# Four edits to the order of transfers and VectorE work in a spectral mixer and token MLP with its backward pass

## The chip, the cores and the metric

The kernel runs on one core of one Trainium2 chip. A core has a matrix engine (TensorE, PE in the profile), a vector engine (VectorE, DVE), a scalar engine (ScalarE, ACT), a general engine (GpSimd, POOL) and a sequencer for transfers (SyncE, SP; its queue is SPq). All transfers of this kernel are issued by SP, in the order of its program: where SP waits before one of them, all later ones wait too. The metric is the device time in microseconds (us) of one execution, lower is better.

## The reference

One layer with two residual blocks, and then the gradients of everything. With x of 2048 x 448 (S x D, bf16):

```python
def _A_ref(x, w_r, w_i):
    X = rfft2(x, axes=(-2, -1))
    X = X * (w_r + 1j * w_i)
    return irfft2(X, s=(S, D)).astype(bfloat16)

def _B_ref(x, w1, b1, w2, b2):
    h = _layernorm(x)
    u = _gelu(einsum("bsd,sf->bdf", h, w1) + b1)
    y = einsum("bdf,fs->bds", u, w2) + b2
    return y.transpose(0, 2, 1)

h = x + _A_ref(_layernorm(x), A_w_r, A_w_i)
h2 = h + _B_ref(_layernorm(h), B_w1, B_b1, B_w2, B_b2)
```

The outputs are h2 and, for a given grad_out, the gradients of x, w_r, w_i (2048 x 225 each), w1 (2048 x 1792), b1, w2 (1792 x 2048) and b2.

## The kernel before

The Fourier transforms are matrix products with sine and cosine matrices that the kernel makes itself. The order of the work on PE, SP, DVE and ACT is the order of the program text; no scheduler moves it. Two helpers bend it. `fill(n)` issues up to n matmuls of a generator that stands in `pending`, so that PE has independent work in a gap. `defer(us, fn)` puts off a transfer's issue until the program has issued that much matmul time. `evac` copies a PSUM result to SBUF on ACT or DVE, whichever has the smaller sum of estimated costs so far (`Meter`).

The stages, in order:

- **Forward rows** (the loop over t up to 16): `row_a` and `row_b` make the transform along D of one row block; after every second `row_b` a reshuffle (L649, 226 KB) moves the result from the partitions of one layout to those of the next, region r2 (`D2`). In between `fill` issues products of `dg_gen`: the 14 products of w2 with grad_out, whose transposed w2 loads (L292) go through a ring of five buffers in rE and rO. From the ninth on (`CAP = 9`) these loads are held back. The loads of W (w_r and w_i, four each, L566) are spread over the last row blocks, two of them held until the next stage.
- **Forward spectrum** (`s2_stage`): 16 groups of rows are transformed along S, in eight pairs `c2`, multiplied by W on DVE (`w_mult`) and transformed back (`s2_inv`). In `make_inv` it also turns the forward matrices into the inverse ones: `gen_inv_s` (UTt, VTt) and `gen_inv_d` (csI, four transposes on PE, four scalings on ACT, four on DVE). `w_place` copies W from its load layout (rB) to the layout of the groups (rG) with `evac`. A `drain` issues what is left of `dg_gen`, then `inv_rows` and the layer norm give h.
- **MLP**: seven blocks of two (jp 0 to 6), each with 32 matmuls into u, then gelu on ACT and DVE: g into rE (`gj`), and in six more DVE operations the gelu's derivative (`om`) times dg into rD, with the sum for the gradient of b1. Then y, 16 blocks t of 14 matmuls: `y_head` for the first three up to j = 12, and `y_tail` on DVE, which adds b2 and h (loaded back from memory, L994) and stores. The results lie in a ring of four PSUM banks.
- **Backward**: 16 products with transposed w1 give dh (`ln_bwd` on ACT and DVE), with the backward rows three blocks behind (`LAG`); `fold_prep` prepares two rows on DVE for `row_a`. `gw_gen` makes the gradient of w2 out of transposed g (rE) and later that of w1 out of transposed h (rB), each read through a ring of three buffers in rst by `st_load` (L1173), stored out of a ring of three buffers in rO. These products are the `fill` of the **backward spectrum** (a second `s2_stage`). The gradient of w1 also needs du (rD) transposed, in four quarter loads (`load_du`, L1146) into r2, the region of the row spectra D2.
- **Last stage**: `inv_rows` with `gx_consumer` gives the gradient of x, while the gradients of W and of w1 are stored.

## Time and profile before

| | us |
|---|---|
| median of 3 runs | 404.02 (402.53 to 405.4) |
| profiled execution, its own time | 401.27 |
| its span (first to last instruction) | 399.5 |
| PE busy | 357.9 (90%) |
| DVE busy | 287.3 (72%) |
| ACT busy | 207.6 (52%) |
| POOL busy | 23.5 (6%) |

The chain of work that ended last consists of PE for 46% of the span, DVE for 33%, transfers for 8% and ACT for 7%. The transfers moved 81.85 MB, and the queue of SP took 81.5% of the time of the core's 16 transfer engines. In the rows of the profile L212 is the helper that issues every matmul and L78 the one that issues nearly every ACT and DVE operation, so an instruction is known by its tiles: `ps_mm<-rC,rE` is a matmul of rE (weights) with rC. Buffer numbers are left out there, so r2, r3, r452, r448 all read `r`.

### The profile page before, as it was taken

Reading aid. Unit: us, or ns where it says so; the run is one execution under the profiler, and the core shown is the slowest. Engines: PE = TensorE matmul, PEld = TensorE weight load, DVE = VectorE, ACT = ScalarE, POOL = GpSimd, SP = SyncE. Lnnn points to the kernel's source line nnn. Section 1 sums busy time; section 2 is a strip of 40 time slices with the busy share of each in tenths; the row PEclk is TensorE's granted clock in tenths of the full one; section 3 lists DMA queues with packets and bytes.
Section 4 is the critical chain, followed back from the end, with each engine's and each line's share of the span. In section 5 each row is a group of like instructions: output and inputs, shape, how many; then the busy total and the mean of one; then the engine's idle time right before and its main releaser. Section 6 shows DMA issues by size and latency. Waiting matters only on the chain.

```text
span 399.5 us, 6226 instructions
## 1 busy us (share of the span) xinstructions
PE 357.9 (90%) x2089; PEld 193.7 (48%) x2089; DVE 287.3 (72%) x737; ACT 207.6 (52%) x438; POOL 23.5 (6%) x96
## 2 busy tenths in 40 slices
PE   0888949789899999899999999899999889899795
PEld 0454626334555555445555666544554335455452
DVE  8999627981694888843249887747999923788784
ACT  4486616763896453413213444535545525777472
POOL 8600000000120000000030000000000000000000
PEclk9999989999999999999999999999999999999899
DMA  8999996337999999797858784496455989997774
GB/s 236 287 148 248 193 187 132 87 94 238 283 292 338 322 294 205 152 262 188 195 121 168 176 167 105 113 279 227 142 168 160 235 242 304 243 221 177 194 212 161
DMA packets 146249, 81.85 MB, mean 205 GB/s; under 512 B 97449, under 2 KB 140457, under 8 KB 145833
## 3 DMA queue, kind: packets, MB, share of 16 engines
q1 hardware_dynamic: 146216, 81.46, 81.5%
q8 instruction: 16, 0.26, 0.3%
q14 instruction: 17, 0.13, 0.1%
HBM read 27.56 MB, written 23.89 MB: 129 GB/s over the span
## 4 chain that ended last, share of the span: by engine, by line
PE 46%; DVE 33%; DMA 8%; ACT 7%; issue 4%; SPq 0%; POOL 0%; DVEq 0%; ACTq 0%; POOLq 0%
PE ps_mm L212 37%; DVE rS L78 10%; PE ps_ff L212 9%; DVE rG L78 6%; DVE r L78 5%; DMA rst<-rB 4%; ACT rG L78 2%; DVE rD L78 2%; DVE stats L78 2%; ACT rO L78 2%; DVE rO L78 2%; DMA out_dram<-r 2%; DMA r<-r 1%; DVE rE L78 1%; DMA rE<-in_B_w_dram 1%
## 5 line engine op out<-in xcount | busy, mean ns | idle before, releaser
L212 PEld LDWEIGHTS <-r 128*128 128x128 bf16 (+1 forms) x568 | 54.7, 106 | 44.0 <-issue 2.3
L212 PEld LDWEIGHTS <-rst 112*128 112x128 bf16 x480 | 46.0, 98 | 54.0 <-issue 6.5
L212 PE MATMUL ps_mm<-r,rst 112*128 112x512 bf16 (+1 forms) x256 | 53.2, 356 | 6.2 <-DVE rO L78 3.1
L212 PE MATMUL ps_mm<-rG,rst 112*128 112x512 bf16 x224 | 53.1, 378 | 1.4 <-DMA rst<-rE 1.4
L78 ACT CAST rO<-ps_mm 128x512 bf16<-128x512 f32 (+1 forms) x64 | 35.3, 562 | 32.5 <-PE ps_mm L212 22.9
L212 PEld LDWEIGHTS <-rS 128*128 128x128 bf16 (+1 forms) x368 | 32.2, 99 | 36.2 <-DVE rS L78 7.9
L78 DVE CAST rO<-ps_mm 128x512 bf16<-128x512 f32 (+1 forms) x56 | 35.3, 643 | 17.9 <-PE ps_mm L212 11.8
L212 PE MATMUL ps_mm<-rD,r 128*128 128x448 bf16 x224 | 44.5, 352 | 0.0
L212 PE MATMUL ps_mm<-rC,rE 128*128 128x448 bf16 x144 | 37.1, 378 | 1.6 <-DMA rE<-in_B_w_dram 1.6
L212 PE MATMUL ps_mm<-rB,r 128*128 128x448 bf16 x160 | 31.2, 352 | 0.1
L78 ACT CAST r<-ps_ff 128x452 bf16<-128x452 f32 x47 | 25.4, 540 | 7.2 <-PE ps_ff L212 7.2
L212 PE MATMUL ps_ff<-csI,rAT 113*128 113x448 bf16 x108 | 25.7, 361 | 2.1 <-ACT rAT L78 1.9
L78 DVE SCALAR_TENSOR_TENSOR r<-ps_mm,b2col,r 128x448 bf16<-128x448 f32 x16 | 10.8, 683 | 22.6 <-PE ps_mm L212 16.4
L78 ACT ACTIVATE r<-ps_mm 128x448 bf16<-128x448 f32 x16 | 8.7, 544 | 30.7 <-PE ps_mm L212 30.7
L212 PE MATMUL ps_mm<-rE,rS 128*128 128x448 bf16 x112 | 21.7, 352 | 1.1 <-DVE rE L78 1.1
L78 ACT ACTIVATE r<-rC 128x448 bf16<-128x448 bf16 x16 | 9.1, 571 | 26.0 <-DMA out_dram<-r 19.3
L78 ACT ACTIVATE rG<-rG 128x896 bf16<-128x896 bf16 x14 | 13.3, 950 | 17.4 <-DVE rG L78 17.1
L78 ACT ACTIVATE rS<-rS 128x452 bf16<-128x452 bf16 x16 | 9.3, 580 | 23.2 <-DVE rS L78 23.1
L212 PEld LDWEIGHTS <-rO 128*128 128x128 bf16 (+1 forms) x165 | 15.6, 98 | 11.3 <-ACT rO L78 0.2
L212 PEld LDWEIGHTS <-rE 128*128 128x128 bf16 x144 | 14.2, 104 | 11.8 <-issue 2.3
L212 PE MATMUL ps_mm<-rC,rO 128*128 128x448 bf16 x80 | 18.9, 352 | 0.0
L78 ACT CAST rS<-ps_ff 128x512 bf16<-128x512 f32 x27 | 15.7, 588 | 4.1 <-PE ps_ff L212 4.1
(161 smaller groups left out, 576.0 us busy)
## 6 DMA issues: line engine op xcount, KB each, us to landing
out_dram<-rO SPq DMA_DIRECT2D x14, 512.0 KB
out_dram<-rO SPq DMA_DIRECT2D x16, 448.0 KB
r<-in_B_w_dram SPq DMA_DIRECT2D x5, 1024.0 KB
r<-r SPq DMA_DIRECT2D x16, 226.0 KB
r<-r SPq DMA_DIRECT2D x32, 113.0 KB
rS<-in_B_w_dram SPq DMA_DIRECT2D x4, 896.0 KB
out_dram<-r SPq DMA_DIRECT2D x32, 112.0 KB
rO<-in_B_w_dram SPq DMA_DIRECT2D x2, 1024.0 KB
```

What stands on the lines that cost most here:

```text
L78: fn(**kw)
L212: nc.tensor.matmul(out, lhsT=lhsT, rhs=rhs, start=start, stop=stop)
```

## The change

- The row product and the reshuffle of the last row block are issued inside the loop, straight after those of the block before; the scalings of `gen_inv_d(1)`, which stood between them, go into the second pair of the spectrum stage. The two loads of w_i that stood in the loop go behind the last reshuffle; so does one w2 load more (`CAP` 8). The fill behind the rows is 20 matmuls, not 10.
- `evac` compares the sums with the cost of this copy added.
- For the last two MLP blocks the six derivative operations of each (and the copy and store of the gradient of b1) are put in a list, and up to three of them are issued behind each y tail.
- The first three transposed loads of g are issued in the dh loop, at its last three blocks, not behind it.
- Of the four quarter loads of du one is issued after every fourth group of the backward spectrum, whose part of r2 is then free, not all four after the last group.

```diff
-CAP = 9
-N_FILL_F = (6, 3, 10, 3, 24, 2)
+CAP = 8
+N_FILL_F = (6, 3, 20, 3, 24, 2)
...
     def evac(out, in_, scale=None):
-        if load[0] <= load[1]:
+        n = int(np.prod(in_.shape[1:]))
+        if load[0] + sc.cost('copy', n, False) <= load[1] + ve.cost('tensor_copy', n, in_.dtype == BF16):
...
-                    if c2 == 1:
-                        gen_inv_d(0)
+                    if c2 in (1, 2):
+                        gen_inv_d(c2 - 1)
...
-                if g_last(c2, i):
-                    after_fwd()
+                if after_fwd is not None and c2 < nh and g % 4 == 3:
+                    after_fwd(g // 4)
...
         row_b(t - 1)
+        if t == NT - 1:
+            row_b(t)
...
-        for _ in range((9, 10, 11, 12, 13, 13).count(t)):
+        for _ in range((9, 10, 11, 12).count(t)):
             next(w_loads)
...
-        if t == 15:
-            gen_inv_d(1)
         fill(N_FILL_F[1])
-    row_b(NT - 1)
...
-            for kind in "TWWTTT":
+            for kind in "TWWWWTTT":
                 if kind == "W":
                     next(w_loads)
                 elif held_w2:
                     held_w2.pop(0)()
...
+        d = Later(ve, om_ops) if jp >= NFB // 2 - 2 else ve
+        d.tensor_scalar(out=om, in0=z, scalar1=-1.0, scalar2=1.0, op0=ALU.mult, op1=ALU.add)
+        d.tensor_tensor(out=om, in0=om, in1=x2, op=ALU.mult)
+        d.tensor_tensor(out=q4(om), in0=q4(om), in1=gj, op=ALU.mult)
+        d.tensor_tensor(out=om, in0=om, in1=hh, op=ALU.add)
...
-    defer(12.0, out_gb1)
+    om_ops.append(lambda: defer(2.0, out_gb1))
...
         y_tail(t, py)
+        for _ in range(3):
+            if om_ops:
+                om_ops.pop(0)()
...
+        if t >= NT - 3:
+            st_load()
...
-    for _ in range(3):
-        st_load()
...
-    s2_stage(bwd_x, bwd_mult, 0, N_FILL_B[3], N_FILL_B[4], False, lambda: [load_du(q) for q in range(4)], 2.0 * INV_SD)
+    s2_stage(bwd_x, bwd_mult, 0, N_FILL_B[3], N_FILL_B[4], False, load_du, 2.0 * INV_SD)
```

Three places in the order of instructions. The first is SP's queue around the end of the forward rows. `r_72<-r_77` is a reshuffle, `rB<-in_A_w_r` and `rB<-in_A_w_i` are loads of W, and a transposed load from `in_B_w` is one of w2. Before, and then after:

```order
L649 DMA r_72<-r_77 16x8x904
L566 DMA rB<-in_A_w_i_dram 64x1x3600
L566 DMA rB<-in_A_w_i_dram 48x1x3600
L649 DMA r_72<-r_77 16x8x904 x2
L292 DMA_TRANSPOSE rO<-in_B_w_dram 128x16x128
L566 DMA rB<-in_A_w_i_dram 16x3375
L566 DMA rB<-in_A_w_i_dram 16x225
L292 DMA_TRANSPOSE rE<-in_B_w_dram 128x16x128 x3
```

```order
L567 DMA rB<-in_A_w_r_dram 16x225
L650 DMA r_72<-r_77 16x8x904 x3
L293 DMA_TRANSPOSE rO<-in_B_w_dram 128x16x128
L567 DMA rB<-in_A_w_i_dram 64x1x3600
L567 DMA rB<-in_A_w_i_dram 48x1x3600
L567 DMA rB<-in_A_w_i_dram 16x3375
L567 DMA rB<-in_A_w_i_dram 16x225
L293 DMA_TRANSPOSE rO<-in_B_w_dram 128x16x128
```

All of w_i and one more w2 load (there are now two into rO behind the reshuffles, before one) moved behind the last three reshuffles.

The second is DVE at the end of the MLP. `rE<-rG` writes g, `rG` alone is gelu work, `ISA rD` the product with dg, and `r_80<-ps_mm,b2col,r_80` is a y tail. Before, and then after:

```order
L78 TENSOR_SCALAR rG<-rG 128x896 x2
L78 TENSOR_TENSOR rE<-rG 128x8x112
L78 TENSOR_SCALAR rG<-rG 128x896
L78 TENSOR_TENSOR rG<-rG 128x896
L78 TENSOR_TENSOR rG<-rG,rE 128x896
L78 TENSOR_TENSOR rG<-rG 128x896
L78 ISA rD,gb_103<-rD,rG 128x4x112
L78 ISA gb_103 128x1
L78 ISA rD,gb_103<-rD,rG 128x4x112
L78 ISA gb_103 128x1
L78 CAST rst<-gb_103 128x14
L78 SCALAR_TENSOR_TENSOR r_80<-ps_mm,b2col,r_80 128x448 x16
```

```order
L78 TENSOR_TENSOR rE<-rG 128x8x112
L78 SCALAR_TENSOR_TENSOR r_80<-ps_mm,b2col,r_80 128x448
L78 TENSOR_SCALAR rG<-rG 128x896
L78 TENSOR_TENSOR rG<-rG 128x896
L78 TENSOR_TENSOR rG<-rG,rE 128x896
L78 SCALAR_TENSOR_TENSOR r_80<-ps_mm,b2col,r_80 128x448
L78 TENSOR_TENSOR rG<-rG 128x896
L78 ISA rD,gb_103<-rD,rG 128x4x112
L78 ISA gb_103 128x1
L78 ISA rD,gb_103<-rD,rG 128x4x112
L78 ISA gb_103 128x1
L78 SCALAR_TENSOR_TENSOR r_80<-ps_mm,b2col,r_80 128x448
```

The derivative work of the last two blocks now stands between the first five y tails.

The third is SP's queue late in the backward spectrum. `r_72<-rD` is a quarter load, `r_73<-r_77` a reshuffle of the inverse, `rst<-` a transposed load for the weight gradients, `out_dram<-rO` a store of one. Before, and then after:

```order
L1195 DMA out_dram<-rO 128x2048
L1146 DMA_TRANSPOSE r_72<-rD 128x14x128 x4
L717 DMA r_73<-r_77 8x16x452
L1173 DMA_TRANSPOSE rst<-rB 128x4x128
L717 DMA r_73<-r_77 8x16x452
L1195 DMA out_dram<-rO 128x2048
```

```order
L1198 DMA out_dram<-rO 128x2048
L1162 DMA_TRANSPOSE r_72<-rD 128x14x128
L716 DMA r_73<-r_77 8x16x452
L1132 DMA_TRANSPOSE rst<-rE 128x4x128
L716 DMA r_73<-r_77 8x16x452
L1198 DMA out_dram<-rO 128x2048
```

One quarter load stands where four stood, and the other three stand earlier in the stage, each between two stores.

More of the change, by code (lines that the diff above doesn't have):

```diff
@@ L1120, with st_load @@
     LAG = 3
+    st_ring = ring(rst, 0, 3, 4, P)
+    order = [(rE, j) for j in range(NFB)] + [(rB, t) for t in range(NT)]
+    ahead = []
+    def st_load():
+        if order:
+            reg, j = order.pop(0)
+            st = st_ring.next()
+            nc.sync.dma_start_transpose(out=st, in_=reg[:, j * 512:(j + 1) * 512])
+            ahead.append(st)
     def rows(t):
```

20 lines of the change are left out of this document (3 added, 17 removed).

## The prediction, made before the changed kernel was run

> **What bounds the kernel now.** I read the waits of TensorE (PE) first, since it is busy for 90% of the span, then the timelines of PE and of the queue of transfers (SPq, issued by SyncE) around each of its waits, then VectorE (DVE) at the same places. In the waits the columns are: engine, line, who was waited for, total us, times, longest.
>
> ```profile
> span 399.5 us, 6226 instructions
> ...
> PE ps_ff L212 <- DVE rX L78: 11.8, 5, 9.3
> PE ps_ff L212 <- DMA r<-r: 5.5, 1, 5.5
> ```
>
> The 9.3 us are the program's start, which the change leaves alone. The next row is one single stop. The PE timeline shows it (start, duration, instruction; in brackets the idle time before it and who ended it), and the chain that ended last shows what lay ahead of it.
>
> ```profile
> 47.16 0.39 PE L530 MATMUL ps_ff<-ident,csF 128*113 128x128 bf16 x4
> ...
> 47.95 0.56 PE L212 MATMUL ps_ff<-csF,rS 112*128 112x226 bf16 x4
> ...
> 50.24 0.39 PE L212 MATMUL ps_ff<-permI,Vt 128*128 128x128 bf16 x4
> 56.17 0.54 PE L212 MATMUL ps_ff<-r,Vt 128*128 128x452 bf16 x1 [5.54 <-DMA r<-r]
> ...
> 60.05 0.35 PE L212 MATMUL ps_ff<-r,Vt 128*128 128x452 bf16 x1
> ```
>
> ```profile
> 49.74 0.55 DVE r L78
> ...
> 50.34 5.74 DMA r<-r
> ```
>
> The last row product (47.95) is cast only at 49.74, behind the inverse-matrix scalings on DVE; its reshuffle leaves at 50.34 and lands 5.74 later. PE has nothing but one product until 56.17. In front of it in the queue stand two loads of W and behind it the next w2 load:
>
> ```profile
> 44.86 1.24 SPq L566 DMA_DIRECT2D rB<-in_A_w_i_dram  x2
> 46.30 4.61 SPq L649 DMA_DIRECT2D r<-r  x2
> 51.00 4.87 SPq L292 DMA_TRANSPOSE rO<-in_B_w_dram  x1
> ```
>
> The stop costs more than its length. The stretch behind it (columns: length; busy us of PE, its weight loads, DVE, ACT, POOL; granted clock; transfer share; GB/s) runs at 0.59 of the clock:
>
> ```profile
> 56.20:60.00 3.80, 3.80 (x20) 2.06 (x21) 1.27 (x4) 1.07 (x2) 0.00 (x0) 0.59 0.91 195
> ```
>
> That is 3.80 x (1 - 0.59) = 1.56 us of PE lost.
>
> **Part 1, the forward spectrum.** Three things move. The last row product is issued straight behind the one before it, at 47.16, so it ends near 47.7; with a cast of 0.55 the reshuffle leaves at 48.3 instead of 50.34. The second half of W and one w2 load stand behind it. Ten more product matmuls (20 instead of 10) stand ahead of the stage; one is 0.20 us by this row (3.00 / 15):
>
> ```profile
> 92.42 3.00 PE L212 MATMUL ps_mm<-rC,rE 128*128 128x448 bf16 x15
> ```
>
> PE stood still from 56.17 - 5.54 = 50.63. Ten products more and four transposes less (0.39) give 50.63 + 2.00 - 0.39 = 52.2 for the stage's earliest start. When does the reshuffle land? At the slow end 5.74 after issue, as now: 54.0. At the quick end three transposed loads of another stage, the first of which PE used 255.21 - 251.93 = 3.3 us after its issue began:
>
> ```profile
> 251.93 4.62 SPq L1173 DMA_TRANSPOSE rst<-rE  x3
> ...
> 255.21 0.60 PE L212 MATMUL ps_mm<-rG,rst 112*128 112x512 bf16 x2 [1.41 <-DMA rst<-rE]
> ```
>
> That gives 51.6. With the big loads gone from in front I take the quick end: start at 52.2, no stop, no slow clock. [...]
>
> What is late next? DVE. It is busy from 62.4 to the stage's last product:
>
> ```profile
> 61.63 0.83 DVE L78 TENSOR_SCALAR csI<-ps_ff,cols 113x112 bf16<-113x112 bf16 x4 [4.17 <-ACT csI L78]
> 62.38 1.15 DVE L78 CAST rX<-ps_ff 128x452 bf16<-128x452 f32 x2
> 63.45 0.68 DVE L78 CAST VTt<-ps_ff 128x512 bf16<-128x512 f32 x1
> ...
> 64.87 3.31 DVE L78 COPY rG<-rB 64x900 bf16<-64x900 bf16 x8
> 68.19 1.17 DVE L78 TENSOR_TENSOR rS<-rX,rG 128x904 bf16<-128x904 bf16 x2
> ```
>
> The first multiplication by W starts 68.19 - 56.17 = 12.0 us after the stage. By the order on DVE it gets ahead of it a second group of scalings (+0.83) and two more casts (+1.15), loses the VTt cast (-0.68), keeps its eight W copies, and no longer waits on a slow PE (-1.56): 11.8. So it starts at 64.0, 4.2 earlier. Behind it two casts fewer (-1.15) against one copy more (+0.41): the stage ends 4.9 earlier. The ten products are missing in the drain at 92.42, which is 2.0 shorter. What the drain covered, the last inverse reshuffle, must then land in 21 x 0.20 = 4.2 us; the quick end above (3.3) fits, and the table load on ScalarE (ACT) behind the drain covers the rest. Sum: -6.9. The w2 load and the last half of W now come late, so I give back 0.6: **-6.3**.
>
> **Part 2, the gelu factors.** Columns as in the timeline; PE first, then DVE.
>
> ```profile
> 159.61 6.97 PE L212 MATMUL ps_mm<-rE,rS 128*128 128x448 bf16 x36
> 167.71 3.94 PE L212 MATMUL ps_mm<-rE,rS 128*128 128x448 bf16 x20 [1.12 <-DVE rE L78]
> 172.02 5.46 PE L212 MATMUL ps_mm<-rE,r 128*128 128x448 bf16 x28 [0.36 <-DVE r L78]
> ```
>
> ```profile
> 161.04 0.39 DVE L78 TENSOR_SCALAR rG<-rG 128x896 bf16<-128x896 bf16 x1
> ...
> 164.54 0.39 DVE L78 TENSOR_SCALAR rG<-rG 128x896 bf16<-128x896 bf16 x1
> ...
> 180.55 0.68 DVE L78 SCALAR_TENSOR_TENSOR r<-ps_mm,b2col,r 128x448 bf16<-128x448 f32 x1 [4.54 <-DMA r<-h_d]
> ```
>
> The six deferred operations of the last block but one take 164.54 - 161.04 = 3.5 us on DVE. PE missed the last gelu block by 1.12, so that wait goes, and with it the 0.36, since the first y tail stands ahead of the deferred work. Behind each of the first five y tails now stand up to three operations (about 1.7 us), less than the 14 matmuls of a block of y (2.7 us, 5.46 / 2), so the four PSUM banks hold. The latest tail is the one at 180.55, set by its load of h and not by DVE. All other y work stays: **-1.5**.
>
> **Part 3, the earlier transposed loads of g.** The 1.41 at 255.21 goes, but PE then runs into the next row product, which needs
>
> ```profile
> 256.05 0.69 DVE L78 TENSOR_TENSOR rS<-rA 128x448 bf16<-128x448 bf16 x2
> ```
>
> ready at 256.7, with or without the load. This wait takes the place of the one removed: **0** (at most -1.4 if I misread what that product needs).
>
> **Part 4, the four quarter loads.** Now they stand together and hold the queue for 7.44 us, with the last reshuffles and the next transposed loads behind them:
>
> ```profile
> 311.92 7.44 SPq L1146 DMA_TRANSPOSE r<-rD  x4
> ```
>
> ```profile
> 323.00 3.20 PE L212 MATMUL ps_mm<-r,rst 112*128 112x512 bf16 x16 [1.02 <-DMA rst<-rB]
> 326.87 2.76 PE L212 MATMUL ps_mm<-r,rst 112*128 112x512 bf16 x12 [0.67 <-DMA rst<-rB]
> ...
> 338.28 1.46 PE L212 MATMUL ps_mm<-r,rst 112*128 112x512 bf16 x8 [0.84 <-ACT rO L78]
> ...
> 372.68 1.25 PE L212 MATMUL ps_mm<-r,rst 112*128 112x512 bf16 x4 [2.13 <-DVE rO L78]
> ```
>
> ```profile
> 336.20 0.76 ACT L78 ACTIVATE rX<-rX,nmr_x,rstd_x 128x448 bf16<-128x448 bf16 x1 [3.09 <-DMA rX<-in_A_x_dram]
> ```
>
> Spread over the stage, each costs the queue 7.44 / 4 = 1.9 us every 11 us, where the transfer engines have half their time free (share 0.50):
>
> ```profile
> 293.00:304.00 11.00, 11.00 (x58) 5.43 (x57) 10.72 (x23) 5.71 (x12) 0.00 (x0) 1.00 0.50 158
> ```
>
> So 1.02 and 0.67 go. The loads of x, which stand behind the same queue, come about 4 us earlier; ACT's 3.09 goes, and PE's 0.84 with it: **-2.5**. The 2.13 at 372.68 hangs on stores of the last stage, which stay: I leave it. If none of these goes, the part is worth 0; if all waits from 319 on go (6.2 us) and the slow clock behind the longest, 1.7 us, with them, it is -7.9. That slow clock:
>
> ```profile
> 370.00:380.00 10.00, 7.87 (x39) 4.05 (x38) 7.42 (x19) 4.59 (x11) 0.00 (x0) 0.83 0.70 188
> ```
>
> Here 10.00 x (1 - 0.83) = 1.7 us went behind a wait of only 2.13. The Trainium skill ("TensorE: Matmul & The Clock Gate", Part 1) says that the clock halves after an idle window of about 3.4 us; by that a wait of 2 us would cost 2 us, by this row 3.8. I go by the row: short waits of PE that the change brings count nearly double.
>
> **Sum.** -6.3 - 1.5 + 0 - 2.5 = -10.3. The profiled execution took 401.27 (span 399.5), so 391.0 there; its own time lies 2.75 below the median of the runs, 404.02, which becomes **393.7**. One per cent, about what a measurement here can tell from no change, is 4.0 us.
>
> **The rivals.** *The reshuffle is slow by itself*: it also lands 5.74 after issue with nothing in front, at 54.0. For it: 16 partitions take it all. Against it: the queue ahead of it is full now. PE then waits 54.0 - 52.2 = 1.8, and the gain is 8.5: 395.5. In this case the reordering of the W loads does nothing, and only the earlier issue and the ten products help.
>
> *The w2 load comes late.* It now leaves behind the last reshuffle, near 48.9. PE wants it at the second pair of rows, 52.2 + (60.05 - 56.17 - 1.56) + 0.6 = 55.1. Under a full queue one such load took from 7.57 to 17.89:
>
> ```profile
> 7.57 6.96 SPq L292 DMA_TRANSPOSE rE<-in_B_w_dram  x1
> ```
>
> ```profile
> 17.89 0.55 PE L212 MATMUL ps_mm<-rC,rE 128*128 128x448 bf16 x2 [1.60 <-DMA rE<-in_B_w_dram]
> ```
>
> At 10.3 it would land at 59.2, a wait of 4.1 and a slow clock of 1.56 behind it: 5.7 of the 10.9 that stand without my allowance are gone, 5.2 stay: 398.8. Against it: the queue holds far less by then.
>
> *The quarter loads stop the stores* (the side slower than before). In the backward spectrum DVE has 10.72 of 11.00 us to do, and its casts write a ring of three output buffers. A quarter load ahead of a store makes that store late, and DVE then waits as it does behind the four today:
>
> ```profile
> 325.47 1.26 DVE L78 CAST rO<-ps_mm 128x512 bf16<-128x512 f32 x2 [3.63 <-DMA out_dram<-rO]
> ```
>
> Four such waits are 14.5 us in a stage that DVE bounds, and part 4 brings nothing: 404.02 - 7.8 + 14.5 = 410.7. It decides once a store is late by more than two tiles of that stage, some 11 us; at half that no DVE wait would show. Against it: transfers have half their time free there.
>
> *The time moves into the next stage*: the earlier forward stage meets the loads of w1, whose queue is full until the MLP. I find no PE wait there today; it would leave parts 2 and 4 alone, 404.02 - 4.0 = 400.0.
>
> **How the numbers follow.** Forecast 0.62, with its own range 391 to 396 (part 3 and more of part 4 on one side, no part 4 on the other). Slow reshuffle 0.14, late w2 load 0.13, next stage 0.06, stopped stores 0.05. Eight times in ten: below, 390.5, for half of the waits that I left in the tail; above, 399.5, which takes in the late w2 load. Faster by over 1% means below 400.0: forecast, slow reshuffle, most of the late load, 0.87; the rest of it and most of the next-stage case, 0.08; slower 0.05.
>
> **What would show it.** Right: PE at the first spectrum product without an idle time above 1 us near 52, its clock near 1.00 there, the drain near 21 products; no wait for rE at the start of y; the wait of 1.41 replaced by one for DVE rS; no wait for rB behind the quarter loads. Wrong: a wait of PE for rO in the first rows of the stage (w2 late), DVE waiting for stores in the backward spectrum, or the last reshuffle still over 5 us. The forecast falls if the forward stage ends less than 4 us earlier.

## The result and the profile after

The changed kernel takes **388.34 us** (median of four runs, 388.02 to 388.41), the kernel before took 404.71 beside it (four runs, 402.53 to 406.12). The ratio is 0.960, with a 95% interval of 0.955 to 0.965. The sign was right, the size was not: 16.4 us were gained where 10.3 were forecast, and the time lies 2.2 us below the forecast's range. The experiments ran on other chips; there the kernel before had medians of 398.8 to 400.4, and the changed kernel took 386.0 where the kernel before took 399.5, so 13.5 us were gained (0.966, 0.959 to 0.973). Four executions among the experiments took 471 to 1595 us; no figure here contains them.

The page of the changed kernel (span; PE's busy time; the clock granted in 40 slices):

```profile
span 386.6 us, 6229 instructions
...
PE 353.7 (91%) x2089; PEld 192.4 (50%) x2089; DVE 286.2 (74%) x738; ACT 207.0 (54%) x437; POOL 24.0 (6%) x96
...
PEclk9999999999999999999999999999999999999999
```

The same row of the kernel before has two slices below 9, behind its two longest stops after the program's start:

```profile
PEclk9999989999999999999999999999999999999899
```

PE's waits after (who, total, times, longest). The reshuffle, 5.5 us in one stop before, is no longer among the large ones:

```profile
PE ps_ff L213 <- DVE rX L78: 12.1, 5, 9.3
PE ps_ff L213 <- ACT rS L78: 6.7, 8, 1.5
PE ps_mm L213 <- DVE rO L78: 3.6, 3, 2.1
```

The forward part in PE's timeline and in that of SP's queue (start, duration, instruction):

```profile
46.76 0.95 PE L213 MATMUL ps_ff<-csF,rS 112*128 112x226 bf16 x8
47.55 4.51 PE L213 MATMUL ps_mm<-rC,rE 128*128 128x448 bf16 x23
51.90 0.39 PE L213 MATMUL ps_ff<-permI,Vt 128*128 128x128 bf16 x4
52.12 0.35 PE L213 MATMUL ps_ff<-r,Vt 128*128 128x452 bf16 x1
```

```profile
42.34 6.54 SPq L650 DMA_DIRECT2D r<-r  x3
48.98 2.23 SPq L293 DMA_TRANSPOSE rO<-in_B_w_dram  x1
```

The stage begins at 52.12, with no idle time in front (56.17 and 5.54 before). DVE sees the reshuffle at 51.58 and starts the first multiplication by W at 64.36:

```profile
51.58 1.31 DVE L78 TENSOR_SCALAR r<-r 128x904 bf16<-128x904 bf16 x4 [0.75 <-DMA r<-r]
...
64.36 1.17 DVE L78 TENSOR_TENSOR rS<-rX,rG 128x904 bf16<-128x904 bf16 x2
```

And the stretch behind the start, at full clock where the other had 0.59 (the eighth column):

```profile
52.10:56.00 3.90, 3.90 (x35) 2.61 (x33) 1.42 (x4) 3.11 (x8) 0.11 (x1) 1.00 1.13 253
```

The start of each part in PE's timeline, by the first product that belongs to it, shows where the 12.9 us between the two profiled executions come from:

| first product of | before | after | earlier by |
|---|---|---|---|
| forward spectrum | 56.17 | 52.12 | 4.05 |
| inverse rows (`RTm`) | 98.28 | 92.20 | 6.08 |
| products on `csI` | 101.05 | 93.28 | 7.77 |
| u | 116.70 | 108.94 | 7.76 |
| y | 159.61 | 151.85 | 7.76 |
| dh | 203.79 | 194.23 | 9.56 |
| backward spectrum | 270.86 | 261.29 | 9.57 |
| last stage (`RTm`) | 329.65 | 317.87 | 11.78 |
| its last row | 382.27 | 369.38 | 12.89 |

Three steps: 7.77 up to the inverse rows, 1.80 in y, 3.3 in the last stage and just ahead of it. The other 3.5 of the 16.4 are in no trace: the kernel before was profiled at 401.27, below all four of its timed runs, and the changed one at 388.41, like its runs.

### The profile page after: what moved, and what is told of

Read it like the earlier page. It is cut to its first block, busy times and chain, and to the rows that moved or that the text cites. A ratio compares the mean times of both kernels' runs of the same rounds, so it can differ in the third digit from the quotient of the medians.

```text
span 386.6 us, 6229 instructions
## 1 busy us (share of the span) xinstructions
PE 353.7 (91%) x2089; PEld 192.4 (50%) x2089; DVE 286.2 (74%) x738; ACT 207.0 (54%) x437; POOL 24.0 (6%) x96
## 4 chain that ended last, share of the span: by engine, by line
PE 58%; DVE 26%; DMA 6%; ACT 4%; issue 4%; SPq 1%; POOL 0%; DVEq 0%; ACTq 0%; POOLq 0%
PE ps_mm L213 50%; DVE rS L78 10%; PE ps_ff L213 8%; DMA out_dram<-r 6%; DVE r L78 5%; DVE stats L78 2%; DVE rO L78 2%; ACT rO L78 2%; DVE rG L78 1%; DVE rX L78 1%; ACT rS L78 1%; DVE rC L78 1%; DVE rA L78 1%; DVE rD L78 1%; ACT csI L78 1%
## 5 line engine op out<-in xcount | busy, mean ns | idle before, releaser
L213 PE MATMUL ps_mm<-r,rst 112*128 112x512 bf16 (+1 forms) x256 | 52.0, 352 | 5.1 <-DVE rO L78 3.6
L78 DVE CAST rO<-ps_mm 128x512 bf16<-128x512 f32 (+1 forms) x57 | 35.1, 629 | 14.7 <-PE ps_mm L213 13.5
L213 PE MATMUL ps_mm<-rC,rE 128*128 128x448 bf16 x144 | 35.6, 367 | 1.5 <-DMA rE<-in_B_w_dram 1.5
L78 ACT CAST r<-ps_ff 128x452 bf16<-128x452 f32 x49 | 26.4, 540 | 6.5 <-PE ps_ff L213 6.5
L213 PE MATMUL ps_ff<-csI,rAT 113*128 113x448 bf16 x108 | 24.9, 353 | 0.4 <-ACT rAT L78 0.2
L78 ACT ACTIVATE r<-rC 128x448 bf16<-128x448 bf16 x16 | 9.1, 571 | 26.7 <-DMA out_dram<-r 13.5
```

The lines of the kernel that those rows point to most:

```text
L78: fn(**kw)
L213: nc.tensor.matmul(out, lhsT=lhsT, rhs=rhs, start=start, stop=stop)
```

## The experiments

Medians are of three to ten runs. The kernel before ran beside each experiment on the same chip, and its time is named where it matters. The changed kernel itself ran on two chips only (388.34 and 386.0). Of its variants, only the order of the loads and the ring stood on the same chip as one of these; the others are compared with 386.0 across chips whose kernels before differ by up to 1.6 us, so that a difference of about 1 us settles nothing there without a trace.

**The kernel before, again**, for the clock of each run.

> The kernel before, unchanged, run again to see the span and the granted clock of each of its runs. Theory A (the long stop of TensorE ahead of the forward spectrum, 5.54 us in the profile, is followed by a clock that differs from run to run; the profile caught a mild case): the times lie 401 to 406 with 3 us or more between the lowest and the highest, the longer runs have the lower mean granted clock (0.99 and less), and the profile shows slices under 1.0 behind the 5.54 us stop and behind the 2.13 us stop near 370. Rival B (the spread has nothing to do with the clock: transfers, or what lies around the span): the same spread at one and the same mean clock. Rival C (the earlier three runs were a chance): all within 1 us of 401.3.

Measured: 400.37 (398.1 to 402.7). Over all experiments the kernel before ran 57 times, at 397.2 to 403.3, and its time goes with the mean granted clock (0.980 to 0.996): the correlation is -0.87. The 12 runs at a clock of 0.995 or more have a mean of 398.1 (397.2 to 398.9), the 11 at 0.983 or less 402.5 (401.1 to 403.3). The changed kernel's runs here had 0.999 to 1.000 and 385.7 to 386.0. In the profile the stretches behind the 5.25 us stop and behind the one of 2.04 us read (clock: eighth column)

```profile
55.40:56.40 1.00, 1.00 (x4) 0.53 (x5) 1.00 (x4) 0.08 (x1) 0.00 (x0) 0.50 1.27 290
...
59.40:60.40 1.00, 1.00 (x12) 0.81 (x11) 0.00 (x0) 0.66 (x2) 0.11 (x1) 0.87 1.13 247
...
372.60:374.60 2.00, 2.00 (x9) 0.94 (x8) 1.89 (x7) 1.04 (x2) 0.00 (x0) 0.77 0.77 140
374.60:376.60 2.00, 2.00 (x11) 1.25 (x10) 1.96 (x6) 1.27 (x4) 0.00 (x0) 0.50 0.84 306
376.60:378.60 2.00, 2.00 (x10) 0.89 (x9) 1.64 (x4) 1.09 (x2) 0.00 (x0) 0.87 0.88 110
```

Half the clock for some 4 us behind the first stop and 3.4 behind the second (0.9 + 2.0 + 0.5, from the shares of the three rows). Theory A holds for the clock, though the times are lower than its 401 to 406; whether the stops cause it is tested below.

**Part 1 alone, and part 1 undone.** `before_new_forward` is the kernel before with these lines new; `after_old_forward` the changed kernel with them old.

```diff
-CAP = 9
-N_FILL_F = (6, 3, 10, 3, 24, 2)
+CAP = 8
+N_FILL_F = (6, 3, 20, 3, 24, 2)
...
-                    if c2 == 1:
-                        gen_inv_d(0)
+                    if c2 in (1, 2):
+                        gen_inv_d(c2 - 1)
...
+        if t == NT - 1:
+            row_b(t)
...
-        for _ in range((9, 10, 11, 12, 13, 13).count(t)):
+        for _ in range((9, 10, 11, 12).count(t)):
...
-        if t == 15:
-            gen_inv_d(1)
...
-    row_b(NT - 1)
...
-            for kind in "TWWTTT":
+            for kind in "TWWWWTTT":
```

> The kernel before with part 1 alone (gen_inv_d at chunk 2, the last row's products and 20 fill products ahead of the second half of the drain, four W loads at once): the long stop at the stage start is gone, all else is as before. Theory A (the stop makes the spread and most of the 3.4 us by which the median lies over the profile): profile about 393.5 (401.3 - 7.8, the shift that the two traces have at the first U product), median within 1 us of the profile, spread under 1 us: the part is worth about 11 in medians. Rival B (spread and offset come from the stop of 2.13 us in the last stage or from elsewhere): profile the same, median 396 to 397.5, spread 2 us and more. My recorded sum: part 1 worth 6.3, median 398.4.

> The changed kernel with part 1 alone undone: the old places of gen_inv_d, row products, fill (10) and W loads. Theory A: the long stop of about 5.5 us and a slowed clock behind it are back, the median is 398 to 400.5 (388.3 + 7.8 + up to 3.4) and the runs differ by 2 us or more. Rival B: the stop is back and costs what the traces show, 6.3 to 7.8: 394.6 to 396.1, with runs within 1 us of each other.

Measured: alone 394.41 beside 399.97, a gain of 5.6 (by the ratio's interval, 3.5 to 8.9; 6.3 were forecast; theory A's 11 and its tight spread are wrong: 391.6 to 394.6). The fastest run had a clock of 1.000, the others 0.993 to 0.996, and the stop of 1.96 near 366 is still there. Undone: 390.72, at clocks of 0.985 to 0.990. Its stop of 5.98 is back, yet it is only 4.7 slower than the changed kernel, less than either theory. The table above explains why in part: the step from 6.08 to 7.77 at the inverse rows stays in this kernel, where the first product on `csI` follows 1.06 after the first `RTm` product (2.77 in the kernel before; below).

**The order of the loads alone** (two loads of w_i, and by `CAP` one w2 load, ahead of the last reshuffle again).

```diff
-CAP = 8
+CAP = 9
...
-        for _ in range((9, 10, 11, 12).count(t)):
+        for _ in range((9, 10, 11, 12, 13, 13).count(t)):
...
-            for kind in "TWWWWTTT":
+            for kind in "TWWTTT":
```

> The changed kernel with the old order of the loads alone (two W loads and a w2 tile ahead of the last reshuffle rows, as before, and the old number of tiles in flight), all else new: gen_inv_d, row products and 20 fill products stay. Theory A (the last reshuffle rows stand on SP behind the loads and land about 56 us, and this alone made the stop): the first product of the forward spectrum at 55.5 to 56.5 with a stop of 3.5 to 4.5 us ahead of it (5.5 less 10 more fill products of 0.19), slices under full clock behind it, time 390.5 to 394. Rival B (the late row products and gen_inv_d on DVE made the stop): start within 1 us of 52.1, stop under 1 us, 388 to 389.

Measured: 391.92 beside 386.0 for the changed kernel on the same chip. SP's queue and PE:

```profile
44.11 1.24 SPq L567 DMA_DIRECT2D rB<-in_A_w_i_dram  x2
45.77 2.63 SPq L650 DMA_DIRECT2D r<-r  x2
48.49 7.11 SPq L293 DMA_TRANSPOSE rO<-in_B_w_dram  x1
```

```profile
51.38 0.39 PE L213 MATMUL ps_ff<-permI,Vt 128*128 128x128 bf16 x4
55.89 0.53 PE L213 MATMUL ps_ff<-r,Vt 128*128 128x452 bf16 x1 [4.13 <-DMA r<-r]
```

The last reshuffle is issued no later than in the changed kernel (its issue is over at 48.4, there at 48.9), but DVE gets it at 55.88, 7.5 us later, and there at 51.58, 2.7 later. So the loads around it on the same queue make it late, not its own issue; which of the three (two of w_i, one of w2) does it, no run separates. This one reordering costs 5.9 us when it is undone, as much as part 1 gains alone. Rival B (the DVE work) is out, and so is the prediction's rival of a reshuffle that is slow by itself. (The edits cannot be added up: all of part 1 undone costs 4.7, less than this order alone.)

**10 instead of 20 fill products in the changed kernel.**

> The changed kernel with 10 instead of 20 fill products behind the last row products: the reshuffle lands as it does now, about 51.5, and TensorE runs out 1.9 us earlier. Theory A (a stop of 1.5 to 2 us is paid by its length alone, or not at all, since the ten products go to the drain): the stop is 1.4 to 1.9, the stage starts at 51.6 to 52.1, no dip of the clock, 386.0 to 387.5. Rival B (a stop of this length drops the clock as the one of 2.0 us at 372 of the kernel before does): a slice of 0.8 to 0.9 near 52 to 62 in the profile or a mean clock under 0.997 in half of the runs, 387.5 to 390.

Measured: 385.04 (384.9 to 385.6), clock 0.996 to 1.000. The stop is 1.18, the stage starts at 51.06, and nothing is slow behind it:

```profile
51.06 0.35 PE L213 MATMUL ps_ff<-r,Vt 128*128 128x452 bf16 x1 [1.18 <-DMA r<-r]
```

This is the mechanism of theory A, with a stop and a time below its ranges (1.4 to 1.9 us, 386.0 to 387.5). In the new order the ten products that the change put there bring nothing: they are missing at the drain, which with them ends in an idle time of 0.36 (and the inverse rows start at 92.20), without them in none (91.29). The profile names no cause for the 0.36. That the last inverse reshuffle, whose issue is over at 89.09, lands then is inferred.

**The last cast of the drain on ACT.**

```diff
-                    evac(out=dgu[:, j, :, :], in_=v4(pg[:, 0:D]))
+                    if j == NFB - 1:
+                        sc.copy(out=dgu[:, j, :, :], in_=v4(pg[:, 0:D]))
+                    else:
+                        evac(out=dgu[:, j, :, :], in_=v4(pg[:, 0:D]))
```

> The changed kernel with the last cast of the forward drain's product forced on ACT, where it stands ahead of the table load, as in the kernel before; the new rule holds for all others. Theory A (this cast, not the start of the stage, made up 1.2 to 1.7 us of the gain in the forward part, since ACT then comes late to the first cast of the inverse rows): a wait of 1.0 to 1.9 for rAT, 1.8 to 2.8 us instead of 1.08 between the first inverse row product and the first product on csI, time 387.0 to 387.8. Rival B (the table load has room, since the drain ends late): 1.08 again, 386.0 within 0.3.

Measured: 387.29, so 1.3 more. Here are the casts and the table load on ACT, of this kernel, of the changed kernel and of the one before:

```profile
91.85 0.53 ACT L78 CAST rD<-ps_mm 128x448 bf16<-128x448 f32 x1 [2.49 <-PE ps_mm L213]
92.39 1.28 ACT L78 ACT_TABLE_LOAD   x1
```

```profile
88.86 0.53 ACT L78 CAST rD<-ps_mm 128x448 bf16<-128x448 f32 x1 [0.41 <-PE ps_mm L213]
89.39 1.28 ACT L78 ACT_TABLE_LOAD   x1
```

```profile
98.48 0.53 ACT L78 CAST rD<-ps_mm 128x448 bf16<-128x448 f32 x1 [5.33 <-PE ps_mm L212]
99.02 1.28 ACT L78 ACT_TABLE_LOAD   x1
```

In the changed kernel the last cast is on DVE, and the load of ACT's table, which the layer norm behind the drain needs, runs while PE still drains. With the cast forced on ACT it stands behind PE's last product, and PE waits for the first cast of the inverse rows:

```profile
94.41 0.93 PE L213 MATMUL ps_ff<-csI,rAT 113*128 113x448 bf16 x4 [1.40 <-ACT rAT L78]
```

The stretch from the first `RTm` product to the first on `csI` is 2.77 before, 1.08 after and 2.25 here. Theory A: this cast makes 1.17 of the 1.69. In the kernel before with part 1 alone, where the cast stands on ACT, the stretch is 2.27, so the other 0.5 comes with part 1's lines.

**The evacuation rule alone old.**

```diff
-        n = int(np.prod(in_.shape[1:]))
-        if load[0] + sc.cost('copy', n, False) <= load[1] + ve.cost('tensor_copy', n, in_.dtype == BF16):
+        if load[0] <= load[1]:
```

> The changed kernel with the old rule for the evacuations alone (the less loaded engine takes it, without the cost of the one at hand), which the prediction put at nothing. Theory A (the rule has little to do with the 1.7 us gained at the end of the drain, where before the last rD cast stood on ACT ahead of the table load): 388.0 to 388.8, the first product on csI with a wait under 0.6 us. Rival B (the rule is what took the last cast off ACT): a wait of 1.5 to 2 us for rAT is back and the time is 389.8 to 390.4.

Measured: 388.01, but from 386.0 to 389.4: unclear. In its trace the first product on `csI` has a wait of 1.01 for rAT and starts 0.7 later than in the changed kernel on a like chip (94.00 against 93.27). The table load stands at 91.97 again, as it does with the cast forced on ACT (92.39): the rule does take the cast off ACT. Neither theory's figures came (a wait under 0.6, or of 1.5 to 2), and what the rule is worth in time, 0 to 2 us, is not settled by these runs.

**Part 2 undone** (all gelu factors ahead of y).

```diff
-        d = Later(ve, om_ops) if jp >= NFB // 2 - 2 else ve
+        d = Later(ve, om_ops) if jp >= NFB // 2 else ve
...
-    om_ops.append(lambda: ve.tensor_copy(out=gb1b[:, 0:NFB], in_=gb1[:]))
+    ve.tensor_copy(out=gb1b[:, 0:NFB], in_=gb1[:])
...
-    om_ops.append(lambda: defer(2.0, out_gb1))
+    defer(12.0, out_gb1)
```

> The changed kernel with part 2 alone undone: all gelu factors of the last two pairs before y, and the store of gb1 as before. My recorded sum: 1.5 longer (1.12 wait for rE at the start of y back, and 0.36 of ACT's wait). What the two traces of before and after show for y alone: 44.18 against 42.38, so 1.8. Theory A (nothing else hangs on it): y takes 44.1 to 44.3 and the time is 387.5 to 387.9 (386.0 + 1.5 to 1.8). Rival B (the longer y moves the row spectra and gives some of it back behind): y longer by 1.8 and the whole by under 1.

Measured: 388.07, 2.1 more; y takes 44.16 again, and the two waits are those of the kernel before:

```profile
159.70 3.94 PE L213 MATMUL ps_mm<-rE,rS 128*128 128x448 bf16 x20 [1.10 <-DVE rE L78]
164.00 4.32 PE L213 MATMUL ps_mm<-rE,r 128*128 128x448 bf16 x22 [0.36 <-DVE r L78]
```

Theory A by the trace; the time lies 0.2 above its range, and the runs differ by 2.9. The 0.3 above my two waits lie in the same stretch, spread over smaller pieces.

**Part 3 undone** (the three loads of g behind the loop).

> The changed kernel with part 3 alone undone: the three first turned loads of g issued behind the loop over dh instead of inside it. My recorded sum: nothing, since the wait for the loads (1.41) stands beside a wait of the same length for the fold on DVE. Theory A: TensorE's stop near 247 is 1.35 to 1.5 again, now ended by the load or by DVE rS, and the time is 385.7 to 386.4. Rival B (DVE's and SP's orders behind it change and the wait adds up): a stop over 2 us, 387 or more.

Measured: 386.04 (385.4 to 388.2), no difference that these runs can tell. The stop near 247, 1.44 for DVE rS in the changed kernel, is one of 1.17 for the load:

```profile
245.35 0.61 PE L213 MATMUL ps_mm<-rG,rst 112*128 112x512 bf16 x2 [1.17 <-DMA rst<-rE]
```

**Part 4 undone** (the four quarter loads together).

```diff
-                if after_fwd is not None and c2 < nh and g % 4 == 3:
-                    after_fwd(g // 4)
+                if after_fwd is not None and c2 < nh and g == NG - 1:
+                    [after_fwd(q) for q in range(4)]
```

> The changed kernel with part 4 alone undone: the four turned loads of the MLP gradient all issued behind the last row spectrum instead of one behind each quarter. My recorded sum: 2.5 longer (rB wait 1.02 and ACT at the last stage's start, and what hangs on them). The two traces show 2.2 between the last inverse product of the spectrum and the first inverse row (10.62 against 8.40) and another 1.1 later in the last stage. Theory A (the loads' issue on SP holds up the turned rows' and the reshuffles' issue behind it): that stretch is 10.4 to 10.8 again, waits of 0.6 to 1.1 on rst<-rB are back near its start, 388.3 to 389.3. Rival B (the stage's length goes by the stores of the gradient rows, which the change did not touch): the stretch is longer by 2.2, the later waits shorter by 1 or more, 386.5 to 387.5.

Measured: 390.00 (389.5 to 391.0), 4.0 more than the 386.0 of the changed kernel; the most of all parts beside the first. SP and PE:

```profile
302.49 7.36 SPq L1162 DMA_TRANSPOSE r<-rD  x4
```

```profile
313.46 3.20 PE L213 MATMUL ps_mm<-r,rst 112*128 112x512 bf16 x16 [0.93 <-DMA rst<-rB]
317.41 2.76 PE L213 MATMUL ps_mm<-r,rst 112*128 112x512 bf16 x12 [0.75 <-DMA rst<-rB]
...
329.72 1.46 PE L213 MATMUL ps_mm<-r,rst 112*128 112x512 bf16 x8 [1.07 <-ACT rO L78]
```

The stretch ahead of the last stage is 10.58 again instead of 8.40. Two waits near it and one on ACT are back, as the prediction's steps and theory A have it. The time lies 0.7 above theory A's range: the last stage takes 50.69, 1.5 more than in the fastest trace of the changed kernel itself but less than in its first (the next two runs).

**The changed kernel again, and a ring of their own for the gradient rows.** In the first profile of the changed kernel the last stage (first to last `RTm` product) takes 51.51, in the kernel with part 1 undone 48.99, though the instructions stand in the same order there. DVE shows the difference: it waits for stores of finished gradient rows to leave their buffer.

```profile
334.32 0.69 DVE L78 SCALAR_TENSOR_TENSOR r<-r,rstd_x,rA 128x448 bf16<-128x448 bf16 x1 [3.10 <-DMA out_dram<-r]
...
338.61 0.69 DVE L78 SCALAR_TENSOR_TENSOR r<-r,rstd_x,rA 128x448 bf16<-128x448 bf16 x1 [1.53 <-DMA out_dram<-r]
```

```profile
333.40 1.90 PE L213 MATMUL ps_mm<-r,rst 112*128 112x512 bf16 x8 [1.46 <-DMA rst<-rB]
339.68 1.02 PE L213 MATMUL ps_mm<-r,rst 112*128 112x512 bf16 x4 [2.10 <-DVE rO L78]
```

The rows share a ring of eight buffers with three temporaries each, so every store has two rows' time to land. The edit:

```diff
     g_out = w_io(W_view_B, out_2, out_3, True)
+    gx_ring = ring(rS, 0, 4, D)
...
-        gx = m448.next()
+        gx = gx_ring.next()
```

> The changed kernel, unchanged, beside the kernels that it is compared with. Its own four runs were 388.0 to 388.4, with 1.46, 2.10, 0.70 and 0.77 us of waits in the last stage. Theory A (the time from the first product of the last stage to its last row, 51.5 us there and 49.0 to 49.5 in two variants whose instructions of that stage stand in the same or nearly the same order, depends on when the stores of the gradient rows land and so differs between runs): 386 to 389, a spread of 1 us or more, and the profile's stage is anywhere from 49 to 52.6. Rival B (those 2 to 2.5 us belong to the kernel): 388.0 to 388.6 again, and 51.3 to 51.7 for the stage.

> The changed kernel with a ring of four buffers of its own (in a region that is free by then) for the rows of the x gradient in the last stage, in place of every fourth of the eight buffers that the layer norm's temporaries use too. In the changed kernel's profile DVE waits 9.2 us in five waits for the stores of these rows to land before it may write the next one; its casts behind that come late, and TensorE waits 2.10, 0.70 and 0.77 us for them. Theory A (this is what set the last stage's length and its scatter): DVE's wait for these stores falls under 2 us, the stage takes 47.5 to 49 us and the time is 384.5 to 386.5, within 0.7 us of each other. Rival B (the stores are late because the queues are full, and TensorE waits for the turned loads instead): the wait on rst grows to 2 us or more and the time stays at 387 to 388.5.

Measured: again 385.97 (385.7 to 386.0), with 49.21 for the stage; the ring 383.19 (382.3 to 383.6), with 45.79. DVE's waits in the last stage, of the changed kernel as first profiled and of the one with the ring:

```profile
DVE r L78 <- DMA out_dram<-r: 9.2, 5, 3.1
```

```profile
DVE r L78 <- ACT r L78: 5.5, 6, 2.5
```

The wait for the stores is gone and with it every PE wait over 0.4 us in the stage. Theory A holds for the cause: DVE waits 9.2 us for these stores in the trace with 51.51 and 6.8 in the one with 49.21, and 2.8 us can be had by giving them room, more than its range (384.5 to 386.5) allowed. Its scatter from run to run did not come: the runs agree within 0.4 us on either chip, so the 2.3 us lie between the two chips, and why the stores land later on one of them is open.

**The kernel before with more fill: 40 products.**

> The kernel before with 40 instead of 10 fill products behind the last row products: the late reshuffle stays, but TensorE has 5.7 us more of products of its own for the time. Theory A (the stop costs twice: once by its length, once by a lower clock behind it, and this cost differs from run to run): the stage starts at 55.5 to 56.5 as before, with a stop under 1 us and full clock; the drain behind the spectrum is shorter by up to 30 products (5.7 us) but what follows it (casts, the table load) takes back some; 393 to 396 and the lower part of the spread of before (398 to 403) is cut, with one more clock dip left in the last stage. Rival B (the clock has no part in it): the same gain of up to 5 us on the profile, but the spread of 3 to 4 us stays.

Measured: 426.77, a failed experiment. By the program's count of matmul time the last inverse reshuffle was now issued behind six loads of weights, where the queue was full:

```profile
93.22 6.95 SPq L910 DMA_DIRECT2D r<-in_B_w_dram  x2
100.26 3.33 SPq L910 DMA_DIRECT2D rO<-in_B_w_dram  x1
103.69 6.65 SPq L957 DMA_DIRECT2D rS<-in_B_w_dram  x2
...
120.41 0.68 SPq L717 DMA_DIRECT2D r<-r  x1
```

```profile
123.09 1.50 PE L212 MATMUL ps_ff<-RTm,r 128*113 128x128 bf16 x12 [30.56 <-DMA r<-r]
```

Its time tells nothing of the clock behind the first stop (in its trace the forward spectrum starts at 55.63 without a stop and at full clock), but it shows that `fill` moves deferred transfers, and what that can cost: 30.56 us.

**With 30 products; with the ring; with both** (all on the kernel before).

> The kernel before with 30 instead of 10 fill products behind the last row products: 3.8 us more of TensorE's own work in the stop of 5.25 to 5.5 us, the late reshuffle and all loads as before. (With 40 the last inverse reshuffle came to stand on SP behind five weight loads of 1 MB; here it stays ahead of them.) Theory A (a long stop is paid twice: its length, and a slower clock behind it that differs from run to run): the stop is 1.3 to 2 us, no slice under 0.9 of the clock near 57, the stage starts at 55.4 to 56.5 as before and its end is at the same place, the drain is 3.8 shorter; time 393.5 to 396, and the spread falls from 5.7 (397.3 to 403.3) to 3 or less, what is left being the dip behind the 2.0 us stop of the last stage. Rival B (the clock's dips have other causes): time 395 to 397, spread 4 us or more, mean clocks 0.98 to 0.996 as before.

> The kernel before with the ring of four buffers for the gradient rows in the last stage and nothing else: the stop of 2.04 to 2.13 us near 372 is to go, the long forward stop stays. Theory A (this stop drops the clock too, in some of the runs): the slice near 370 to 380 has full clock, the stage is 48 to 49.5 instead of 52.6, the median is 395 to 397 and the spread 3 to 4 (what the forward stop alone makes). Rival B (in the kernel before the late turned loads set the last stage, not the stores of the rows): waits on rst take the place, stage over 51, median 398 to 399.5.

> The kernel before with both of its stops cut: 30 fill products ahead of the forward spectrum (1.49 us of stop instead of 5.25) and the ring of four buffers in the last stage (no stop of 2 us). Each alone left a spread of 3.2 to 3.8 us and mean clocks of 0.987 to 1.0. Theory A (the spread and the offset of the kernel before are the slower clock behind these two stops and nothing else): all runs at a mean clock of 0.997 or more and within 1.2 us of each other, median 390.5 to 392.5 (400.3 less 4.6 less 3.7, give or take what the two have in common). Rival B (the clock's dips come at any stop, or without one): a spread of 2.5 us or more, clocks down to 0.99.

| | median | runs | mean clocks |
|---|---|---|---|
| kernel before beside the first two | 400.33 | 398.0 to 402.7 | 0.980 to 0.996 |
| 30 products | 395.72 | 394.4 to 397.7 | 0.991 to 1.000 |
| ring | 396.62 | 395.4 to 399.2 | 0.987 to 0.995 |
| both | 393.19 | 391.4 to 394.3 | 0.996 to 1.000 |

In the first, the forward stop is 1.49 with full clock behind it:

```profile
55.38 0.35 PE L212 MATMUL ps_ff<-r,Vt 128*128 128x452 bf16 x1 [1.49 <-DMA r<-r]
```

```profile
55.00:60.00 5.00, 4.62 (x36) 3.03 (x37) 2.80 (x10) 2.70 (x7) 0.11 (x1) 1.00 0.95 200
```

With both stops cut no run is under a mean clock of 0.996 (0.997 was named): the clock's part of theory A holds. But shorter stops can bring half the clock too: in the trace with 30 products a stop of 1.66 ahead of the inverse rows is followed by it (last section). The second half of theory A does not hold: the median lies above its 390.5 to 392.5, and a spread of 2.9 us stays with clocks of 0.996 to 1.000. What makes that is open; the transfers' landing times in the last stage are a candidate, but there the ring had already been put in.

**Two ways to a better kernel.** With the ring, 8 of the 40 fill products that stand behind the backward rows moved ahead of the last two of them, to cover the wait of 1.44 for DVE rS; and then 10 forward fill products too.

```diff
     for t in range(NT - LAG, NT + 2):
+        if t == NT - 2:
+            fill(8)
         rows(t)
-    fill(N_FILL_B[2])
+    fill(N_FILL_B[2] - 8)
```

> The changed kernel with the ring of four buffers for the gradient rows, and 8 of the 40 fill products that stood behind the row products of the backward spectrum moved ahead of the last two of them, where TensorE waits 1.44 us for the fold on DVE. Theory A (8 products of 0.22 us cover the wait, and the 32 left still cover the last reshuffle): no wait over 0.5 near 247, the forward part of the backward spectrum starts with no stop, 381.6 to 382.2 (383.2 less 1.0 to 1.5). Rival B (the 40 products were needed behind the rows: the last reshuffle lands no earlier, and the wait moves there): a stop of 1.4 us ahead of the first spectrum product, 383 to 383.6.

> The changed kernel with three edits that each gained alone: the ring of four buffers for the gradient rows, 8 fill products ahead of the last two backward row products, and 10 instead of 20 fill products ahead of the forward spectrum. If they add up: 381.7 less 0.9 to 1.0, so 380.5 to 381, all runs within 1 us at full clock. If the ten products are needed in the drain where the other edits have moved nothing, the same. Against it: the stop of 1.2 us that they leave drops the clock in some runs, 382 to 384 in those.

Measured: 381.64 (381.2 to 381.7), 0.957 of the kernel before (0.954 to 0.960), and 381.62 (380.9 to 382.4). The first does what it was to do: dh to the backward spectrum takes 65.65 instead of 67.06. The second adds nothing: the forward spectrum's inverse begins earlier, but the inverse rows start at 91.78, against 91.52 without it. The changed kernel with the ring and the eight products is the best here, 4.3 us below the changed kernel by the medians and 3.6 by the two ratios to the kernel before (0.966 and 0.957).

## Why the prediction was right or wrong

Every sign that the prediction named for its forecast came (no idle time at 52.12, full clock there, 21 products in the drain, no wait for rE, one for DVE rS, none for rB ahead of the last stage), and the time still lies outside its range. What failed are sizes, and one step that was carried over.

- **Part 1 by itself was right**: 6.08 up to the inverse rows in the trace, 5.6 as a part alone, against 6.9 before my allowance and 6.3 after. Its pieces came near too: first product 52.12 (52.2), first W multiplication 64.36 (64.0). The drain gave 1.4 instead of 2.0, probably since the last inverse reshuffle ended it and not the products (inferred). The late w2 load and the late W, for which I gave back 0.6, cost nothing: PE used the tile at 54.86 without a wait. Of its edits, the order of the loads is the one that counts (5.9 when undone); the ten products, which the sum counted at 2.0, bring nothing in this order.
- **The first mis-sized term: the end of the forward drain.** The sum had the table load as cover for the last reshuffle, and no term at all for the new evacuation rule. The rule put the drain's last cast on DVE, so the load ran at 89.39, while PE still drained, and not behind the drain as at 99.02. The step is 1.69 us in the trace; the cast alone makes 1.17 of it, the rule undone gives back 0.7 in its trace. The prediction had read no row of ACT there.
- **Part 2 was right** (1.80 in the trace, 2.1 in medians, for 1.5), and **part 3** exactly so: nothing, with the wait for DVE rS in place of the other, as said.
- **The second mis-sized term: part 4**, 3.3 in the traces and 4.0 undone, for 2.5. The three waits were the right ones, and the stretch ahead of the last stage gave 2.2. The rest lies in the last stage, which I left as it was: I set the 2.13 at 372 aside as untouched, and with it the slow clock of 1.7. That stage takes 52.6 in five traces of the kernel before and its variants without the ring, each with half the clock behind a stop of about 2 us, and 49.0 to 51.5 in nine traces of the changed kernel and its variants without the ring and with part 4. Part 4 undone takes 50.69, which lies within these, so how much of it is part 4 stays open. (In the trace after, a stop of 2.10 stands at 339.7 without a slow clock: the prediction's rule that short waits count nearly double fails there.) The rival of stopped stores in the backward spectrum fell: DVE waits for none there.
- **The step that failed most: "its own time lies 2.75 below the median of the runs ... which becomes 393.7".** I carried the offset over unchanged, and it went. Of the miss of 5.4 (393.7 less 388.34) this is 2.75, the terms above are 2.6. The prediction had measured the slow clock behind both stops in one execution (1.56 and 1.7 us) and spent it as if every execution had the same. How much half clock a stop brings differs between executions: two stretches of 3.4 us in the profiled execution of the kernel before, three in its second profile. So this kernel scatters by 6 us with its clock, and taking both stops away takes the low clocks away. That the offset of those first four runs was a low clock is inferred: their clocks are not recorded, and they ran on another chip, where the changed kernel, too, was 2.3 us slower. On the chip of the second measurement, where 13.5 us were gained, the forecast's 10.3 falls short by 3.2, and the mis-sized terms are most of that.
- The range was too narrow on the side of a gain. It held half of the waits left in the tail, but neither the offset's loss nor a gain from a rule for casts.

## What to carry to other kernels

When the profile shows a long stop of PE, price it as its length plus the half clock behind it, which differs from one execution to the next, and do not carry the offset of a median over its profile to a kernel from which the stop is gone. A small transfer on which a stage hangs must be ahead of the big ones on the queue, not merely issued at the same time (2.7 us against 7.5 here). And look at who does the last cast ahead of a table load, and how many rows a store has before its buffer is wanted again: they were worth 1.2 and 2.8 us here, and the prediction argued over neither.

## What was not expected of the hardware

The clock behind a stop is half, and then full again, in one step. Behind the long stops it is half from the first product on: for 3.1 us after 4.13 us of stop, 4.3 after 5.25, 5.6 after 30.56. Near 2 us of stop it comes late or not at all: after 2.04 (above) and 1.91 PE first runs at full clock for 1.2 us, and then at half for 3.4; after the 2.10 in the changed kernel nothing follows, but after the 1.66 with 30 products something does. So the length of the stop does not decide.

The traces show what does. From the first entry of the clock record on (11 to 15 us into each of the 20 traces), every change of the clock lies a whole multiple of 3.413 us behind that entry. Cut at these marks, the traces have 2151 whole stretches at full clock. In 14 of them PE is without work for 1.89 us or more, and half clock follows in all 14; in the other 2137 it is without work for at most 1.87 us, and half clock follows in none. (The ends of PE's work are modelled in a trace, so the limit is good to some hundredths.) Of 25 stretches at half clock, the 11 with 1.23 us or more without work are followed by another, the 14 with 0.35 or less by full clock. Three pairs of such stretches, around the 1.91 of the kernel with part 3 undone, the 1.66 of the kernel before with 30 products and the 2.10 of the changed kernel (the time without work is 3.41 less the third column, PE's busy time; the clock is the eighth column):

```profile
336.83:340.24 3.41, 1.50 (x9) 0.67 (x7) 2.27 (x7) 0.81 (x3) 0.00 (x0) 1.00 0.50 136
340.24:343.65 3.41, 3.41 (x13) 1.66 (x12) 3.27 (x9) 2.10 (x5) 0.00 (x0) 0.50 1.50 202
...
92.94:96.35 3.41, 1.52 (x17) 1.11 (x17) 0.00 (x0) 3.30 (x6) 0.00 (x0) 1.00 0.98 375
96.35:99.76 3.41, 3.41 (x17) 2.00 (x16) 1.87 (x5) 1.57 (x5) 0.43 (x2) 0.50 0.98 281
...
338.03:341.44 3.41, 1.76 (x11) 0.95 (x11) 2.76 (x8) 0.70 (x2) 0.00 (x0) 1.00 0.59 178
341.44:344.85 3.41, 3.41 (x26) 2.01 (x24) 2.94 (x8) 2.94 (x7) 0.00 (x0) 1.00 1.33 141
```

Without work: 1.91, 1.89 (the 1.66 and a second wait of 0.23) and 1.65, since a mark cuts the 2.10 in two. So a stop of about 2 us brings 3.4 us of half clock, up to 1.7 us of PE's work, or nothing, by where it lies between the marks, and the marks lie elsewhere in each execution. By these numbers (an estimate: twice 1.89) a stop of 3.8 us always brings it. The Trainium skill ("TensorE: Matmul & The Clock Gate", Part 1) has a window of 3.4 us that runs freely beside the kernel, and the clock halved after an idle one. The marks agree with such a window; that 1.89 of its 3.4 us without work are enough does not follow from the page, and the rows decide.
